# Attention and token/channel mixer: transposing u of batches 1 to 3 by DMA instead of on TensorE

## The chip, the cores and the metric

The kernel runs on one core of one Trainium2 chip. The metric is the device time of one execution in microseconds (us). Times of before: 226.68, 228.03 and 229.67 us in three runs, median 228.03. The profiled execution took 226.8 us.

Engines are named as in the profile: PE (TensorE), PEld (its weight loads), DVE (VectorE), ACT (ScalarE), POOL (GpSimd), SP (SyncE, which here only issues DMAs).

## The reference, cut

```python
# q, k, v: (4, 8, 768, 64); attention with 4 sink tokens and a window of 128
scores = scale * np.matmul(q, k.transpose(0, 1, 3, 2))
...
keep = is_sink | in_window
...
x = softmax(scores) @ v                 # then (4, 768, 512): batch, token, channel
xt = x.transpose(0, 2, 1)
h = np.maximum(xt @ w_tok1, 0.0) @ w_tok2
u = x + h.transpose(0, 2, 1)            # token mixing, residual
h2 = np.maximum(u @ w_ch1, 0.0) @ w_ch2
out = u + h2                            # channel mixing, residual; float32
```

## The kernel before, in words

There are 4 batches, and 16 pairs of heads, four pairs to a batch. Tokens are in 6 tiles of 128, channels in 4 tiles of 128. Each pair is loaded (load_qk, L75, from SP; load_v, L101, from POOL), cast to bf16 on POOL, transposed on PE, scored against its band and its sinks, put through exp on ACT, masked on DVE and multiplied with v (pv, L415). The result is x_sb, with tokens on the partitions.

Token mixing (mix_h, L474, and mix_u, L500) is done in two groups of channels: group 0 is the first 384 channels (three pairs of heads), group 1 the last 128 (the last pair). mix_u makes, for a token tile, two matmuls of 384 or 128 columns in PSUM (tag "mx", three banks), and DVE adds x (L513) and writes u_sb in bf16, with tokens on the partitions.

Channel mixing needs u with channels on the partitions: uT, a tile of 128 x 4 x 768. transpose_u (L522) makes it: PE transposes blocks of 128x128 of u_sb into PSUM (L114), and ACT or DVE copies them to uT (L118, L120). In a batch this is 24 blocks and 8 copies. Then mix_channels (L569) forms v1T = relu(w_ch1^T uT) in 12 tiles of channels and two halves of tokens of 384 each (a "half" is token tiles 0 to 2 or 3 to 5), four matmuls of 384 columns for each, one for each tile of channels; and then, per token tile, 12 matmuls of 512 columns with w_ch2 (out_part, L591), an addition of u on DVE (L603), and a store from SP (L606). u_sb, uT and h1T lie in two buffers, o_sb in three.

The order of the work is planned when the program is built. Plan (L223) keeps a clock for PE, ACT and DVE from written costs, and lets two streams of PE units run against each other: main is the channel mixing of batch b, side the attention and token mixing of batch b + 1. At each step it takes from the side stream if that is behind target(m) (L684), which says how much of the side should be done when main has come to m: before, all of it at 0.95 of main's stage. Every instruction is then kept in the planned order on its engine. Dependencies across engines, and for DMAs, are semaphores. A DMA has a lane of eight, and waits for the one that used that lane before it.

SP's queue is thus in planned order too: q and k loads, output stores, each behind the one before it. A store waits on SP for its addition on DVE. The loads of a pair are issued when the pair four earlier is through (load_next, L632).

The batch boundary is where main goes from batch b to b + 1: the 12 matmuls of mix_u of group 1 for batch b + 1, what is left of out_part for batch b and of attention for batch b + 2, then the first v1 of batch b + 1, which reads uT.

Of the kernel before, what the change touches and what calls it, by code (L numbers as in the profile page):

```python
# [16 lines left out]
def kernel(  # L17
# [13 lines left out]
    nc = tc.nc  # L31
    B, H, S, D = q.shape
    P = 128
    NT = S // P
# [5 lines left out]
    NTOK = DTOK // P  # L40
# [20 lines left out]
    in_order = tc.keep_in_program_order  # L61
# [66 lines left out]
    def load_w(out, in_):  # L128
# [15 lines left out]
        out=ident, in_=ident, compare_op=ALU.not_equal, fill=1.0, base=0, pattern=[[-1, P]], channel_multiplier=1,  # L144
    ))
    for i in range(2):
        in_order(nc.gpsimd.affine_select(
            out=mask_main[:, i, 0], in_=mask_main[:, i, 0], compare_op=ALU.is_ge,
# [3 lines left out]
            out=mask_main[:, i, 1], in_=mask_main[:, i, 1], compare_op=ALU.is_ge,  # L152
# [13 lines left out]
    for n in range(NKB):  # L166
        e = (nc.vector, nc.gpsimd)[n]
# [7 lines left out]
        out=mask_add, in0=mask_main, scalar1=-1.0, scalar2=30000.0, op0=ALU.add, op1=ALU.mult,  # L175
# [26 lines left out]
    for n in range(NW):  # L202
        ch1_last = load_ch1(n)

    class Op:
        def __init__(self, cost, fn, deps=(), tag=None, then=(), size=0.0):  # L210
            self.cost, self.fn, self.deps, self.tag, self.then = cost, fn, list(deps), tag, list(then)
            self.done = None
            self.size = size

    def landed(at):
# [1 line left out]
        op.done = at  # L217
        return op

    SEM = 90.0  # L220
    PE_OUT = 190.0

    class Plan:  # L223
        def __init__(self):
            self.free = {"PE": 0.0, "ACT": 0.0, "DVE": 0.0}
            self.pending = []
            self.rings = {t: [None] * n for t, n in TAGS.items()}
            self.turn = {t: 0 for t in TAGS}
# [43 lines left out]
        def run(self, main, side, target):  # L272

            main, side = list(main), list(side)
            m = s = 0.0
            while main or side or self.pending:
                o = self.other()
                tm = self.start_pe(main[0]) if main else None
                ts = self.start_pe(side[0]) if side else None
                pick = None  # L280
                if tm is not None and ts is not None:
                    behind = s < target(m)
                    if behind:
                        pick = "side" if ts <= tm + 40.0 else "main"
                    else:
                        pick = "main" if tm <= ts + 40.0 else "side"
                elif tm is not None:
                    pick = "main"
                elif ts is not None:
                    pick = "side"  # L290
                t = {"main": tm, "side": ts, None: None}[pick]
                if o is not None and (t is None or o[0] <= t):
                    op = self.pending.pop(o[1])
                    op.fn(o[2])
                    self.free[o[2]] = o[0] + op.cost[o[2]]
                    op.done = self.free[o[2]] + SEM
                    continue
                assert pick, "no unit can begin"
                if pick == "main":
                    op = main.pop(0)  # L300
                    m += op.size
                else:
                    op = side.pop(0)
                    s += op.size
                self.commit_pe(op, t)
# [10 lines left out]
    done = {}  # L316
    tiles = {}
# [149 lines left out]
    GROUPS = ((0, DM - P), (DM - P, P))  # L467
# [6 lines left out]
    def mix_h(b, g, t0, n):  # L474
        c0, cn = GROUPS[g]

        def run():
            if ("mix", b) not in tiles:
                tiles["mix", b] = (
                    mix_pool.tile([P, NTOK, DM], BF16, name="h1T"),  # L480
                    mix_pool.tile([P, NT, DM], BF16, name="u_sb"),
                    mix_pool.tile([P, NC, S], BF16, name="uT"),
                )
            ps_h = tiles["ps_h", b, g, t0] = bank("mx", n, cn)
            for tt in range(n):
                for st in range(NT):
                    mm(
                        ps_h[:, tt], w_tok1[:, st, ts(t0 + tt, P)], x_sb[b][:, st, c0:c0 + cn],
                        start=(st == 0), stop=(st == NT - 1),
                    )  # L490

        w = n * cn
        op = Op(
            {"ACT": 190.0 + 0.78 * w, "DVE": 150.0 + 1.05 * w},
            lambda e: relu(e, tiles["mix", b][0][:, t0:t0 + n, c0:c0 + cn], tiles["ps_h", b, g, t0]),
        )
        done.setdefault(("h", b, g), []).append(op)
        return unit(n * NT * cn * 0.422, run, of_group(b, g) + [done["tok1"]], "mx", [op])

    def mix_u(b, g, s0, n):  # L500
        c0, cn = GROUPS[g]

        def run():
            ps_u = tiles["ps_u", b, g, s0] = bank("mx", n, cn)
            for st in range(n):
                for tt in range(NTOK):
                    mm(
                        ps_u[:, st], w_tok2[:, tt, ts(s0 + st, P)], tiles["mix", b][0][:, tt, c0:c0 + cn],
                        start=(tt == 0), stop=(tt == NTOK - 1),
                    )  # L510

        def add(e):
            in_order(nc.vector.tensor_tensor(  # L513
                out=tiles["mix", b][1][:, s0:s0 + n, c0:c0 + cn], in0=tiles["ps_u", b, g, s0],
                in1=x_sb[b][:, s0:s0 + n, c0:c0 + cn], op=ALU.add,
            ))

        op = Op({"DVE": 150.0 + 1.05 * n * cn}, add)
        done["u", b, g, s0] = op
        return unit(n * NTOK * cn * 0.422, run, done["h", b, g] + [done["tok2"]], "mx", [op])  # L520

    def transpose_u(b, g, s0, n):  # L522
        ct0, nct = GROUPS[g][0] // P, GROUPS[g][1] // P

        def run():
            ps_ut = tiles["ps_ut", b, g, s0] = bank("tr", nct, n * P, dtype=BF16)
            for ct in range(nct):
                for st in range(n):
                    transpose(ps_ut[:, ct, ts(st, P)], tiles["mix", b][1][:, s0 + st, ts(ct0 + ct, P)])

        w = nct * n * P
        op = Op(
            {"ACT": 190.0 + 0.78 * w, "DVE": 150.0 + 0.52 * w},
            lambda e: copy(e, tiles["mix", b][2][:, ct0:ct0 + nct, s0 * P:(s0 + n) * P], tiles["ps_ut", b, g, s0]),
        )
        done.setdefault(("uT", b), []).append(op)
        return unit(nct * n * 56, run, [done["u", b, g, s0]], "tr", [op])

    def attention_and_tokens(b):
        p0 = b * NHP  # L540
        units = [transpose_q(p0), transpose_k(p0)]
        for p in range(p0, p0 + NHP):
            last = p == p0 + NHP - 1
            units += [score(p, 0), score(p, 1)]
            if not last:
                units.append(transpose_q(p + 1))
            if p > p0:
                units.append(pv(p - 1, 0))
            units += [score(p, 2), score(p, 3)]
            if not last:  # L550
                units.append(transpose_k(p + 1))
            units.append(score(p, 4))
            if p > p0:
                units.append(pv(p - 1, 1))
            units += [score(p, 5), score_sinks(p)]

            units[-1].then.append(sink_rows(p))
        units += [mix_h(b, 0, 0, 1), pv(p, 0), mix_h(b, 0, 1, 1), pv(p, 1)]
        for st in range(NT):
            units.append(mix_u(b, 0, st, 1))  # L560
            if st >= 2:
                units.append(transpose_u(b, 0, st - 2, 1))
        units += [
            mix_h(b, 1, 0, NTOK), transpose_u(b, 0, NT - 2, 1), mix_u(b, 1, 0, 4), transpose_u(b, 0, NT - 1, 1),
            mix_u(b, 1, 4, 2), transpose_u(b, 1, 0, 4), transpose_u(b, 1, 4, 2),
        ]
        return units

    def mix_channels(b):  # L569
# [84 lines left out]
    plan = Plan()  # L654
    plan.free.update(PE=3000.0, ACT=2200.0, DVE=3900.0)
    raw0 = raws.pop(0)
    for n, (name, at) in enumerate((("q_bf", 3900.0), ("k_bf", 5100.0))):
        done[name, 0] = Op(
            {"DVE": 550.0, "ACT": 830.0},
            lambda e, n=n: copy(e, bfs[0][n].rearrange("p j h d -> p h j d"), raw0[n]), [landed(at)],  # L660
# [23 lines left out]
    def target(m):  # L684
        m -= first
        total = 0.0
        for n, (msize, ssize) in enumerate(sizes):
            begin = 0.2 if n == 0 else 0.0
            f = (m / msize - begin) / (0.95 - begin)
            if f < 1.0 or n == B - 1:  # L690
                return total + max(0.0, min(1.0, f)) * ssize if m < msize else total + ssize
            if m < msize:
                return total + ssize
            total += ssize
            m -= msize
        return total

    plan.run(main, side, target)


# [33 lines left out]
```

## Time and profile before

| | |
|---|---|
| median of three runs | 228.03 us |
| profiled execution, own time | 226.8 us |
| its span, first to last instruction | 225.1 us |
| PE busy | 206.8 us of the span, 92% |
| DVE, ACT busy | 134.0 us, 128.1 us |
| granted TensorE clock | 1.00 |
| chain that ended last | PE 79%, DMA 10%, DVE 5%, ACT 2% |
| boundaries: first v1 of batch 1, 2, 3 | about 90, 140 and 190 us |

A span of an execution is cut in views: busy time of each engine in a stretch; groups of instructions with count, busy time and the mean length of one; the chain, which follows the last instruction back through whatever released each step; waits; and DMA issues with the time to landing. Matmuls on PE are pipelined, so the length of one is more than the step from one to the next. Rows of the SP queue give the time for which an issue held the queue.

### The profile page before, as it was taken

How to read it: one execution, taken by the hardware profiler on the slowest of the kernel's cores; microseconds unless marked ns; L12 is line 12 of the kernel's file. 1: busy time of each engine (PE TensorE's matmuls, PEld its weight loads, DVE VectorE, ACT ScalarE, POOL GpSimd, SP SyncE). 2: the span in 40 equal slices, each digit the busy share in tenths (PEclk: the TensorE clock that was granted, in tenths of full speed). 3: DMA queues.
4: the chain of work that ended last, by engine and by line, in shares of the span. 5: the costliest groups of instructions: out<-in, count | busy, mean ns of one | idle time of the engine just before them, and what ended most of it. 6: DMA issues, size and time to landing. Idle time of an engine off the chain costs nothing.

```text
span 225.1 us, 4435 instructions
## 1 busy us (share of the span) xinstructions
PE 206.8 (92%) x1770; PEld 132.5 (59%) x1788; DVE 134.0 (60%) x308; ACT 128.1 (57%) x259; POOL 53.1 (24%) x70
## 2 busy tenths in 40 slices
PE   1687896999999999999999999999999999999993
PEld 0455654666766656667766566667765566565441
DVE  5378975029899684499995554599964645000231
ACT  2687944689777522888884023889975022775000
POOL 8798461423045151001341600000000000000000
PEclk9999999999999999999999999999999999999999
DMA  6999999998088792670558921100001211100222
GB/s 198 302 192 154 205 185 260 259 212 260 24 127 171 145 296 60 194 272 4 35 38 153 150 98 47 48 3 0 3 0 50 85 56 50 47 0 0 96 93 93
DMA packets 41781, 26.24 MB, mean 117 GB/s; under 512 B 25888, under 2 KB 38688, under 8 KB 41760
## 3 DMA queue, kind: packets, MB, share of 16 engines
q0 software_dynamic: 29600, 7.08, 33.1%
q1 hardware_dynamic: 12160, 18.88, 25.1%
q8 instruction: 14, 0.23, 0.4%
q14 instruction: 7, 0.06, 0.1%
HBM read 26.74 MB, written 6.29 MB: 147 GB/s over the span
## 4 chain that ended last, share of the span: by engine, by line
PE 79%; DMA 10%; DVE 5%; ACT 2%; issue 1%; POOL 1%; SPq 0%; POOLq 0%
PE ps_mx L111 61%; PE ps_sc L111 8%; PE ps_tr L114 6%; DMA w_ch<-in_moe_w_ch_dram 5%; PE ps_pv L111 4%; DMA q_f<-in_q_dram 3%; DMA k_f<-in_k_dram 2%; DVE o_sb L603 1%; ACT kTz L118 1%; DVE pT L390 1%; DVE kTz L120 1%; ACT pT L384 1%; DVE x_sb L442 0%; POOL q_bf L95 0%; POOL w_ch L129 0%
## 5 line engine op out<-in xcount | busy, mean ns | idle before, releaser
L111 PE MATMUL ps_mx<-w_ch,v1T 128*128 128x512 bf16 x272 | 69.3, 379 | 1.1
L111 PE MATMUL ps_mx<-uT,w_ch 128*128 128x384 bf16 x384 | 69.6, 326 | 0.1
L384 ACT ACTIVATE pT<-ps_sc 128x512 bf16<-128x512 f32 x84 | 46.6, 565 | 10.7 <-PE ps_sc L111 9.3
L111 PEld LDWEIGHTS <-w_ch 128*128 128x128 bf16 x384 | 36.9, 98 | 21.5
L124 ACT ACTIVATE v1T<-ps_mx 128x384 bf16<-128x384 f32 x69 | 33.8, 490 | 12.7 <-PE ps_mx L111 11.9
L111 PEld LDWEIGHTS <-v1T 128*128 128x128 bf16 x288 | 27.0, 98 | 23.6 <-issue 0.7
L603 DVE TENSOR_TENSOR o_sb<-ps_mx,u_sb 128x512 f32<-128x512 f32 x24 | 16.6, 691 | 36.1 <-PE ps_mx L111 34.3
L111 PE MATMUL ps_sc<-qT,kTz 128*128 128x256 bf16 x168 | 31.0, 270 | 4.0 <-DVE kTz L120 1.7
L104 POOL DMA_DIRECT2D v_aug<-in_v_dram x16 | 16.8, 1049 | 58.2 <-PE ps_sc L111 35.7
L390 DVE TENSOR_TENSOR pT<-pT,mask_main 128x512 bf16<-128x512 bf16 (+1 forms) x68 | 29.2, 438 | 0.9
L111 PEld LDWEIGHTS <-kTz 128*128 128x128 bf16 x192 | 17.6, 101 | 14.8 <-DVE kTz L120 3.9
L118 ACT ACTIVATE uT<-ps_tr 128x384 bf16<-128x384 bf16 (+2 forms) x18 | 9.0, 502 | 29.6 <-PE ps_tr L114 29.6
L126 DVE TENSOR_SCALAR v1T<-ps_mx 128x384 bf16<-128x384 f32 x27 | 14.9, 556 | 13.3 <-PE ps_mx L111 12.9
L513 DVE TENSOR_TENSOR u_sb<-ps_mx,x_sb 128x384 bf16<-128x384 f32 (+2 forms) x32 | 16.7, 552 | 6.7 <-PE ps_mx L111 6.5
L111 PEld LDWEIGHTS <-w_tok 128*128 128x128 bf16 x192 | 14.6, 98 | 7.3 <-issue 0.8
L111 PEld LDWEIGHTS <-pT 128*128 128x128 bf16 x352 | 16.9, 97 | 3.1 <-issue 0.9
L118 ACT ACTIVATE kTz<-ps_tr 64x768 bf16<-64x768 bf16 x22 | 17.6, 799 | 1.2 <-PE ps_tr L114 1.0
L111 PE MATMUL ps_pv<-v_aug,pT 128*128 128x65 bf16 x304 | 16.4, 194 | 0.0
L95 POOL CAST q_bf<-q_f 128x768 bf16<-128x768 f32 x15 | 12.9, 863 | 12.3 <-DMA q_f<-in_q_dram 12.3
L442 DVE TENSOR_TENSOR x_sb<-ps_pv,recip 128x384 bf16<-128x384 f32 x28 | 15.5, 552 | 0.3
L111 PE MATMUL ps_mx<-h1T,w_tok 128*128 128x384 bf16 (+1 forms) x96 | 14.9, 272 | 0.5 <-ACT h1T L124 0.3
L120 DVE COPY qT<-ps_tr 128x768 bf16<-128x768 bf16 x12 | 11.5, 956 | 5.8 <-PE ps_tr L114 5.7
(57 smaller groups left out, 197.5 us busy)
## 6 DMA issues: line engine op xcount, KB each, us to landing
q_f<-in_q_dram SPq DMA_DIRECT2D x16, 384.0 KB, 5.8
k_f<-in_k_dram SPq DMA_DIRECT2D x16, 384.0 KB, 6.4
out_dram<-o_sb SPq DMA_DIRECT2D x24, 256.0 KB, 2.0
v_aug<-in_v_dram POOLq DMA_DIRECT2D x16, 192.0 KB, 6.5
w_ch<-in_moe_w_ch_dram POOLq DMA_DIRECT2D x8, 384.0 KB, 11.7
w_tok<-in_moe_w_tok_dram POOLq DMA_DIRECT2D x2, 384.0 KB, 5.8
```

The costliest lines, as they stand in the source:

```text
L104: d = in_order(nc.gpsimd.dma_start(out=v_aug.rearrange("p i t d -> p (i t) d")[:, :, 0:D], in_=v[b].rearrange("h s d -> (h s) d")[2 * hp * ...
L111: in_order(nc.tensor.matmul(*args, skip_group_check=True, **kwargs))
L114: in_order(nc.tensor.transpose(out, in_, ident))
L118: in_order(nc.scalar.activation(out, in_, AF.Copy))
L120: in_order(nc.vector.tensor_copy(out=out, in_=in_))
L124: in_order(nc.scalar.activation(out, in_, AF.Relu))
L126: in_order(nc.vector.tensor_scalar_max(out=out, in0=in_, scalar1=0.0))
L384: in_order(nc.scalar.activation(tiles["pT", p][:, kt, :, 0:nq], tiles["ps_s", p, kt][:, :, 0:nq * P], AF.Exp, scale=scale,))
L390: in_order(nc.vector.tensor_tensor(out=pt, in0=pt, in1=msk[:, :, 0:nq], op=ALU.mult))
L442: in_order(nc.vector.tensor_tensor(out=x_sb[b][:, ts(half, QH), ts(hp, 2 * D)].rearrange("p t (i d) -> p t i d", i=2), in0=tiles["ps_o", p ...
L513: in_order(nc.vector.tensor_tensor(out=tiles["mix", b][1][:, s0:s0 + n, c0:c0 + cn], in0=tiles["ps_u", b, g, s0], in1=x_sb[b][:, s0:s0 + n ...
L603: in_order(nc.vector.tensor_tensor(out=o_sb, in0=tiles["ps_out", b, st], in1=tiles["mix", b][1][:, st], op=ALU.add,))
```

## The change

For batches 1 to 3 transpose_u is replaced by transfer_u: per group and token tile one transposing DMA from u_sb to uT, issued from SP. Its PE units and copies go. Batch 0 is as before. The plan gets a clock for SP, a written cost of 500 ns for an issue and a lag of 2500 ns until uT counts as there. The side stream's target is now 0.85 of main's stage in place of 0.95. The two orders on PE are the same up to the token mixing of batch 1.

```diff
+    DMA_LAG = 2500.0
...
-            self.free = {"PE": 0.0, "ACT": 0.0, "DVE": 0.0}
+            self.free = {"PE": 0.0, "ACT": 0.0, "DVE": 0.0, "SP": 0.0}
...
-                    op.done = self.free[o[2]] + SEM
+                    op.done = self.free[o[2]] + op.lag
...
+    def transfer_u(b, g, s0, n):
+        ct0, nct = GROUPS[g][0] // P, GROUPS[g][1] // P
+        for st in range(s0, s0 + n):
+            def run(e, st=st):
+                _, u_sb, uT = tiles["mix", b]
+                in_order(nc.sync.dma_start(
+                    out=uT[:, ct0:ct0 + nct, ts(st, P)], in_=u_sb[:, st, ts(ct0, P)] if nct == 1 else
+                    u_sb[:, st, ct0 * P:(ct0 + nct) * P], transpose=True,
+                ))
+
+            op = Op({"SP": 500.0}, run, [done["u", b, g, s0]], lag=DMA_LAG)
+            done.setdefault(("uT", b), []).append(op)
+            plan.pending.append(op)
...
-        for st in range(NT):
-            units.append(mix_u(b, 0, st, 1))
-            if st >= 2:
-                units.append(transpose_u(b, 0, st - 2, 1))
-        units += [
-            mix_h(b, 1, 0, NTOK), transpose_u(b, 0, NT - 2, 1), mix_u(b, 1, 0, 4), transpose_u(b, 0, NT - 1, 1),
-            mix_u(b, 1, 4, 2), transpose_u(b, 1, 0, 4), transpose_u(b, 1, 4, 2),
-        ]
+        if b == 0:
...
+        else:
+            for st in range(NT):
+                units.append(mix_u(b, 0, st, 1))
+                transfer_u(b, 0, st, 1)
+            units.append(mix_h(b, 1, 0, NTOK))
+            for s0, n in ((0, 4), (4, 2)):
+                units.append(mix_u(b, 1, s0, n))
+                transfer_u(b, 1, s0, n)
...
-            f = (m / msize - begin) / (0.95 - begin)
+            f = (m / msize - begin) / (0.85 - begin)
```

In the changed program's order, SP has for each of the batches 1 to 3 six transposing DMAs of 128x384 (group 0) and six of 128x128 (group 1). For batch 1: six of group 0, three of group 1, the store of output tile 5 of batch 0, three of group 1, the store of tile 6, then loads. For batches 2 and 3: two of group 0, the store of tile 3 of the batch before, four of group 0, the store of tile 4, two of group 1, the store of tile 5, four of group 1, the store of tile 6. Between the last mix_u and the first matmul that reads uT, PE has 18 w_ch matmuls before each batch, and before batches 1 and 2 also transposes and scores of the next batch's attention.

More of the change, by code (lines that the diff above doesn't have):

```diff
@@ L203, with __init__ @@
         ch1_last = load_ch1(n)
+    SEM = 90.0
+    PE_OUT = 190.0
+    DMA_LAG = 2500.0
     class Op:
-        def __init__(self, cost, fn, deps=(), tag=None, then=(), size=0.0):
+        def __init__(self, cost, fn, deps=(), tag=None, then=(), size=0.0, lag=None):
             self.cost, self.fn, self.deps, self.tag, self.then = cost, fn, list(deps), tag, list(then)
             self.done = None
+            self.lag = SEM if lag is None else lag
             self.size = size
@@ L218, in landed @@
         return op
-    SEM = 90.0
-    PE_OUT = 190.0
     class Plan:
         def __init__(self):
-            self.free = {"PE": 0.0, "ACT": 0.0, "DVE": 0.0}
+            self.free = {"PE": 0.0, "ACT": 0.0, "DVE": 0.0, "SP": 0.0}
             self.pending = []
@@ L558, in attention_and_tokens @@
         units += [mix_h(b, 0, 0, 1), pv(p, 0), mix_h(b, 0, 1, 1), pv(p, 1)]
-        for st in range(NT):
-            units.append(mix_u(b, 0, st, 1))
-            if st >= 2:
-                units.append(transpose_u(b, 0, st - 2, 1))
-        units += [
-            mix_h(b, 1, 0, NTOK), transpose_u(b, 0, NT - 2, 1), mix_u(b, 1, 0, 4), transpose_u(b, 0, NT - 1, 1),
-            mix_u(b, 1, 4, 2), transpose_u(b, 1, 0, 4), transpose_u(b, 1, 4, 2),
-        ]
+        if b == 0:
+            for st in range(NT):
+                units.append(mix_u(b, 0, st, 1))
+                if st >= 2:
+                    units.append(transpose_u(b, 0, st - 2, 1))
+            units += [
+                mix_h(b, 1, 0, NTOK), transpose_u(b, 0, NT - 2, 1), mix_u(b, 1, 0, 4), transpose_u(b, 0, NT - 1, 1),
+                mix_u(b, 1, 4, 2), transpose_u(b, 1, 0, 4), transpose_u(b, 1, 4, 2),
+            ]
+        else:
+            for st in range(NT):
+                units.append(mix_u(b, 0, st, 1))
+                transfer_u(b, 0, st, 1)
[3 more added lines that the diff above has]
+                transfer_u(b, 1, s0, n)
         return units
```

## The prediction

> **What bounds the kernel now.** I read the busy shares first, then the busy times of three stretches, one per batch boundary to the next, then the chain around two boundaries, then the rows for DMA issues. The first view says which engine is full over the whole span, the second whether it is full where the change acts.
>
> ```profile
> PE 206.8 (92%) x1770; PEld 132.5 (59%) x1788; DVE 134.0 (60%) x308; ACT 128.1 (57%) x259; POOL 53.1 (24%) x70
> ```
>
> ```profile
> 40.15:91.43 51.28, 50.59 (x452) 33.10 (x455) 33.81 (x74) 33.01 (x69) 16.82 (x19) 1.00 0.82 166
> 91.43:141.63 50.20, 49.74 (x441) 32.56 (x445) 35.83 (x81) 29.82 (x61) 10.45 (x12) 1.00 0.53 111
> 141.63:189.00 47.37, 47.02 (x419) 30.86 (x422) 32.62 (x79) 28.80 (x59) 0.00 (x0) 1.00 0.09 33
> ```
>
> Each row is a stretch, its length, then busy us of PE, its weight loads, DVE, ACT, POOL, then the granted clock (1.00 all through), DMA share and GB/s. Of 148.85 us PE is idle for 0.69 + 0.46 + 0.35 = 1.5 us. So PE bounds all three, and whatever leaves PE's stream there shortens the span, as long as no new wait comes in. The removed transposes lie there:
>
> ```profile
> L114 PE MATMUL ps_tr<-ident,u_sb 128*128 128x128 bf16 x72 | 7.9, 219 | 0.4 <-DVE u_sb L513 0.4
> ```
>
> A mean of 219 ns is the length of one, but they are pipelined; what one costs is its step in the chain. This is the chain before the last boundary (start, length, what):
>
> ```profile
> 184.47 1.24 PE ps_mx L111 x5
> 185.71 0.17 PE ps_tr L114 x3
> 185.87 1.09 PE ps_mx L111 x11
> 186.97 0.17 PE ps_tr L114 x3
> 187.14 0.87 PE ps_mx L111 x7
> 188.01 0.22 PE ps_tr L114 x4
> 188.23 0.65 PE ps_mx L111 x3
> 188.88 0.11 PE ps_tr L114 x2
> 188.99 17.11 PE ps_mx L111 x103
> ```
>
> Three transposes take 0.17, four 0.22, two 0.11 us: 56.5 ns each. The same view prices the matmuls: 0.216 us for one of 512 columns (three: 0.65), 0.163 for 384, 56.5 ns for 128. All copies of uT are over before the 103 matmuls begin, and PE waits for none. The DMA rows I use (shortest/median/longest ns on the SP queue, then us to landing), first the output stores, then the loads of q and k:
>
> ```profile
> L606 SPq DMA_DIRECT2D out_dram<-o_sb x24: 332/333/360, 64.7 to 222.2; - x24
> DMA to landing us min/median/max: 2.0/2.0/5.3
> ```
>
> ```profile
> L81 SPq DMA_DIRECT2D q_f<-in_q_dram x16: 367/420/1068, 0.8 to 119.7; - x16
> L81 SPq DMA_DIRECT2D k_f<-in_k_dram x16: 397/455/997, 1.3 to 120.2; - x16
> DMA to landing us min/median/max: 3.0/6.3/9.4
> ```
>
> **The change, part by part.** *Removed.* Batches 1 to 3 lose 4 x 6 transposes each, 72 in all, with weight loads that run beside PE: 72 x 56.5 ns = 4.07 us off PE's chain. Their 24 copies (uT rows of 0.29 to 0.60 us) leave ACT and DVE; since PE was idle for only 1.5 us in the three stretches, their absence can give 1.5 us at the very most, and I count nothing.
>
> *Added.* 36 transposing DMAs on SP: per batch six of 128x384 (group 0) and six of 128x128 (group 1). None is in the trace, so two numbers are unknown: I, the time that one holds the SP queue, and L, from issue to landing. Bounds: I from 0.33 (store) to 1.07 us (longest load); L from 2.0 (stores, which also read SBUF) up to 5.3 (longest store), and below 2.0 is possible, since nothing here is written to HBM. I take I = 0.46 (loads) and L = 2.0, the row nearest in source and size: DMA is light around the two later boundaries (0.19 in that column from 129 to 140.5 us and from 178.7 to 190), and 0.78 around the first, where the loads of 74.7 to 77 us are landing. Small packets speak for a longer L: in the software queue 29600 packets took 33.1% of 16 engines, 40 ns each. If a transpose moves rows of 256 bytes one by one, 128x128 makes 8 per engine (0.3 us) and 128x384 makes 24 (1.0 us): small beside 2.0.
>
> *What waits.* PE is in order. In the changed order the first matmuls of a batch wait for uT: half 0 for the token tiles 0 to 2, half 1 for tiles 3 to 5, the fourth matmul of each for group 1. Group 1's DMAs are the last, and SP is in order too: the store of output tile 5 stands among them, and waits for its addition on DVE. Set t = 0 at the start of the first eight group-1 matmuls of mix_u. Before, at the last boundary, the addition behind eight of them starts 0.65 us after they start and takes 0.69: 1.34. The second addition (0.42) ends at 1.76. The twelve matmuls end at 0.68.
>
> - Boundary before batch 3: 18 matmuls of w_ch follow (3.89), nothing else, as no attention is left. Needed: half 0 at 0.68 + 3.89 + 0.49 = 5.06, half 1 at 5.71. Tile 5 is summed after six of the 18, at 1.98; addition 0.2 later, to 2.87; store issued 2.92 to 3.25; then four transposes (tiles 2 to 5). Tile 2 lands at 3.25 + L = 5.25, tile 5 at 3.25 + 3I + L = 6.63. PE waits 0.2, and then 6.63 - 5.9 = 0.7: **0.9 us**.
> - Before batch 2: the same store, but PE has 6 w_ch, 12 transposes of q and k, 12 w_ch, 4 scores, 6 transposes, 2 scores = 5.57 us. Needed 6.74 and 7.39; landing 5.25 and 6.63. Covered, by 0.8 us.
> - Before batch 1: 5.37 us of such work, needed 6.54 and 7.19. Six transposes of q go ahead of tile 5's last matmuls, so its store ends at 3.6 and three transposes follow: 3.6 + 2I + L = 6.5. Covered, by 0.7 us.
>
> So only the last boundary pays, and the other two start to pay at about 0.8 us more.
>
> *Moved: the second edge at boundary 1.* Before, transposes filled PE while DVE added u:
>
> ```profile
> 80.49 2.41 DVE L513 TENSOR_TENSOR u_sb<-ps_mx,x_sb 128x384 bf16<-128x384 f32 x5
> 81.10 0.34 PE L114 MATMUL ps_tr<-ident,u_sb 128*128 128x128 bf16 x3 [0.43 <-DVE u_sb L513]
> ```
>
> Now twelve matmuls of mix_u stand in one row there. They have three banks, and a bank is freed at DVE's pace, 2.41 / 5 = 0.48 us, while two matmuls take 0.33. Pairs 4 to 6 and the mix_h behind them start at 81.10, 81.58, 82.07 and 82.54: 1.44 us for 0.98 us of work. I charge 0.5 us. At the other boundaries w_ch matmuls stand between, and I charge nothing.
>
> *Moved: SP and side stream.* On SP, loads of q and k for batch 3 stand behind batch 1's transposes, but behind the store of tile 6 in both orders, so they leave at about the same time. Group 0's DMAs come one per 0.48 us, from t = -3.5 at boundary 1 (where the chain has the first addition end at 81.05), and need 0.46: no backlog. The target 0.85 packs the attention of batches 2 and 3 tighter (that of batch 1 keeps its order). PE was idle there for 0.6 us outside the boundaries; doubling half of that I charge as 0.3 us; the ends are 0 and 3.
>
> **Sum:** 226.8 - 4.07 + 0.9 + 0.5 + 0.3 = 224.4 us against the profiled execution's own time of 226.8 (span 225.1 and 1.7 around it). The runs of before were 226.68, 228.03 and 229.67, so this execution was near the fastest, 1.2 under the median. I add half of that: 225.0.
>
> **The rivals.**
> *Landing or issue is longer (the other side).* Place: the DMAs behind the store of tile 5 and the first group of v1T. With I kept at 0.46, the three waits are 3.25 + 3I + L - 5.71, the same - 7.39, and 3.6 + 2I + L - 7.19, in sum 3L - 6.5. Without them the change is worth 4.07 - 0.5 - 0.3 = 3.3 us, so it is level at L = 3.3 and slower by 2% (4.5 us) at L = 4.8. A longer I weighs more: at I = 1.0, group 0 of boundary 1 ends at -3.5 + 6 = 2.5, three of group 1 at 5.5, the store at 5.8 and the last lands at 7.8 + L; at the other two the store goes at 3.37 and the last lands at 6.7 + L. With L = 2.0 the waits are 2.6 + 1.3 + 3.0 = 6.9, the time 226.8 - 3.3 + 6.9 = 230.4; with L = 3.0 (shortest load) 233.4; with L = 5.3, 240. For it: loads took up to 1.07 us on SP and never landed under 3.0. Against: those came from HBM in bursts, at a DMA share of 0.82 in the first of the three stretches.
> *Transposes run one at a time.* If each must land before the next, at 2.0 us, group 0 alone takes 12 us. At boundary 1 (start t = -3.5) the twelfth ends at 20.5 and PE waits 13.3 us; at the other two four of group 0 begin at t = -5.3 and end at 2.7, and six more end at 14.7: waits of 7.3 and 9.0. Time: 226.8 - 3.3 + 29.6 = 253. For it: nothing in this trace. Against: ordinary DMAs on SP overlap, loads leave every 0.5 us and land after 6. The Trainium skill, "VectorE: DVE Perf Modes", section "The three transpose paths", gives 390 ns for a 128x128 on TensorE and 1309 ns by DMA, and its rules for authors choose TensorE where PSUM will do as the target. TensorE's is 219 ns in this trace; the DMA's is shown by no run yet. By that page 24 blocks one after another would be 31 us a batch, the waits of this rival 44 us and its time 268 (an estimate from the page).
> *Everything is hidden and the freed DVE and ACT help too.* No wait at the boundaries, and the 1.5 us of idle PE gone: 226.8 - 4.07 - 1.5 = 221.2. Against: the store of tile 5 holds the last four back by its own addition even if L is short.
>
> That the change does not do what it says can be left out: PE has 72 transposes less in the changed order.
>
> **How the numbers follow.** Forecast 0.55 (222.7 to 227), longer landing or issue 0.27 (226.8 to 240, two thirds of it over 2%), one at a time 0.08, all hidden 0.10 (six of ten over 2%). About 2% is what a measurement of this kernel can tell from no change. Faster by over 2%: 0.06. Slower: 0.18 + 0.08 = 0.26. Within: 0.68. The range 222 to 238 leaves out "one at a time", the longest landings and the best of the hidden case, under 2 in 10.
>
> **What would show it.** The transposes' rows on SP give I and L at once. PE's group for u_sb should have 24 transposes left. PE's idle time before its uT matmuls, put down to the transposing DMA, should be near 1 us, nearly all of it before batch 3; 0.5 us should be put down to DVE's u_sb before batch 1. I am wrong if a wait for uT shows before each batch, if I is above 1 us, or if SP's stores keep DVE's additions waiting.

## The result, and the profile after

The changed kernel took 249.02 us (median of 4 runs, 248.03 to 250.33) against 228.85 for the kernel before in the same job (4 runs, 226.68 to 230.96): a ratio of 1.092, interval 1.080 to 1.104. It is slower, and far above the forecast of 225.0. The profiled execution after took 249.82 us, its span 248.1.

From part 1 and part 2 of the page of after, PE's busy time and the granted clock over the span:

```profile
PE 212.6 (86%) x1699; PEld 131.2 (53%) x1716; DVE 130.9 (53%) x292; ACT 121.9 (49%) x251; POOL 53.2 (21%) x70
...
PEclk9999997999999998599999999799999996599999
```

PE has 72 transposes less to do (71 fewer matmul records) and is busy for 5.8 us *more* (206.8 before). The second line says why. In before all forty digits are 9:

```profile
PEclk9999999999999999999999999999999999999999
```

In after there are lower ones: the 7 at about 40 us lies in the start (on which below), but 85, 7 and 65 lie where the batches change. Some of PE's work ran at a lower clock.

The wait that the prediction priced at 0.9 us, from the waits of after (who, for what: sum us, times, longest):

```profile
PE ps_mx L111 <- DMA uT<-u_sb: 16.3, 6, 3.4
```

The rows of the new DMAs, from the view of their source line (hold of the SP queue in ns: shortest, median, longest; then us from issue to landing):

```profile
L530 SPq DMA_TRANSPOSE uT<-u_sb x36: 1099/1213/2387, 82.5 to 208.5; - x36
...
DMA to landing us min/median/max: 2.2/2.4/6.0
```

So I, the hold, is 1.21 us, where the prediction took 0.46 and an upper bound of 1.07; L, the landing, is 2.4 us, where it took 2.0. The chain of after at the boundary before batch 1 (start, length, what) shows what that does:

```profile
94.26 0.52 SPq L632
94.79 0.04 issue
94.83 1.11 SPq L530
95.94 0.04 issue
95.98 1.23 SPq L530
97.22 0.04 issue
97.26 2.33 DMA uT<-u_sb
99.59 0.04 issue
99.63 3.04 PE ps_mx L111 x9
```

SP works without a pause: the store (L632), then transposes 1.2 us apart, and PE starts 0.04 us behind the landing of the last one. A landing of 2.33 us is longer than the hold, so the next transpose leaves before the last one has landed; what PE waits for is the sum of the holds and one landing. The same place on PE (start, length, instructions, idle time before them and its releaser):

```profile
95.47 0.81 PE L111 MATMUL ps_mx<-uT,w_ch 128*128 128x384 bf16 x4 [2.93 <-DMA uT<-u_sb]
99.63 3.04 PE L111 MATMUL ps_mx<-uT,w_ch 128*128 128x384 bf16 x9 [3.35 <-DMA uT<-u_sb]
```

The other four waits are 1.10 and 3.04 us before batch 2, 3.40 and 2.49 before batch 3: per boundary 6.3, 4.1 and 5.9. Nine matmuls of 384 columns took 3.04 us, 0.34 each, where the trace of before had 0.163. The next view, busy time in stretches of after, shows it (stretch, length, busy us of PE, PEld, DVE, ACT, POOL, granted clock, DMA share, GB/s):

```profile
97.60:104.40 6.80, 4.77 (x17) 2.54 (x18) 0.00 (x0) 2.49 (x5) 0.00 (x0) 0.50 0.68 220
155.60:159.00 3.40, 3.40 (x12) 1.72 (x13) 0.00 (x0) 1.36 (x3) 0.00 (x0) 0.50 0.15 55
206.80:217.00 10.20, 7.39 (x23) 3.27 (x23) 0.00 (x0) 2.76 (x6) 0.00 (x0) 0.50 0.12 35
```

Right at or behind each wait the clock is 0.50, for 6.8, 3.4 and 10.2 us. PE was busy for 4.77 + 3.40 + 7.39 = 15.6 us in them; at full clock half of that would do, so 7.8 us are lost. Of these, 0.7 cost nothing. Before batch 3 four of the slow matmuls run ahead of the last wait, and at full clock PE would only have waited that much longer for the last landing:

```profile
207.12 1.44 PE L111 MATMUL ps_mx<-uT,w_ch 128*128 128x384 bf16 x4 [3.40 <-DMA uT<-u_sb]
```

So the half clock adds 7.8 - 0.7 = 7.1 us to waits that would be 16.3 + 0.7 = 17.0 at full clock.

**The account.** The first 80 us differ between executions whose PE order is the same up to there (the fourth output store was issued at 79.9 us before and 81.4 after), so I compare the *rest*: from that issue to the end of the span. Before it is 145.2 us, after 166.7, in the traces 21.5 more. Of that: -4.07 for the 72 transposes, +16.3 waits for uT, +7.8 half clock, +0.4 for DVE's pace at boundary 1: 20.4. About 1 us stays unassigned. The 0.4 is read here:

```profile
82.53 1.41 PE L111 MATMUL ps_mx<-h1T,w_tok 128*128 128x384 bf16 x6 [0.43 <-DVE u_sb L515]
83.92 0.83 PE L111 MATMUL ps_mx<-x_sb,w_tok 128*128 128x128 bf16 x12
```

From 82.53 to 83.92 are 1.39 us for six matmuls that are 0.98 us of work. The idle 0.43 ahead of them is no part of it: it stands in before as well.

Medians below are of all executions and ratios of undisturbed ones alone; the profiled execution of store_on_act was a disturbed one, so of it only waits and issue times are read.

### The profile page after: what moved, and what is told of

Read it like the earlier page. It is cut to its first block, busy times and chain, and to the rows that moved or that the text cites. A ratio compares the mean times of both kernels' runs of the same rounds, so it can differ in the third digit from the quotient of the medians.

```text
span 248.1 us, 4335 instructions
## 1 busy us (share of the span) xinstructions
PE 212.6 (86%) x1699; PEld 131.2 (53%) x1716; DVE 130.9 (53%) x292; ACT 121.9 (49%) x251; POOL 53.2 (21%) x70
## 4 chain that ended last, share of the span: by engine, by line
PE 71%; DMA 12%; SPq 8%; DVE 3%; ACT 2%; issue 2%; POOL 1%; POOLq 0%
PE ps_mx L111 56%; PE ps_sc L111 7%; SPq L530 7%; DMA w_ch<-in_moe_w_ch_dram 5%; PE ps_pv L111 4%; PE ps_tr L114 4%; DMA q_f<-in_q_dram 3%; DMA uT<-u_sb 3%; DVE o_sb L629 2%; DMA k_f<-in_k_dram 2%; ACT kTz L118 1%; SPq L632 1%; DVE kTz L120 1%; ACT pT L386 1%; DVE k_bf L120 0%
## 5 line engine op out<-in xcount | busy, mean ns | idle before, releaser
L111 PE MATMUL ps_mx<-uT,w_ch 128*128 128x384 bf16 x384 | 78.7, 353 | 16.3 <-DMA uT<-u_sb 16.3
L111 PE MATMUL ps_mx<-w_ch,v1T 128*128 128x512 bf16 x273 | 67.2, 379 | 1.0
L111 PEld LDWEIGHTS <-w_ch 128*128 128x128 bf16 x384 | 39.1, 105 | 43.5 <-issue 26.1
L629 DVE TENSOR_TENSOR o_sb<-ps_mx,u_sb 128x512 f32<-128x512 f32 x24 | 16.6, 691 | 49.7 <-PE ps_mx L111 49.6
L111 PEld LDWEIGHTS <-kTz 128*128 128x128 bf16 x192 | 18.1, 101 | 17.0 <-DVE kTz L120 4.0
L124 ACT ACTIVATE h1T<-ps_mx 128x384 bf16<-128x384 f32 (+1 forms) x12 | 5.5, 455 | 32.3 <-PE ps_mx L111 32.3
L515 DVE TENSOR_TENSOR u_sb<-ps_mx,x_sb 128x384 bf16<-128x384 f32 (+2 forms) x32 | 16.1, 550 | 8.7 <-PE ps_mx L111 8.7
L118 ACT ACTIVATE kTz<-ps_tr 64x768 bf16<-64x768 bf16 x19 | 15.2, 800 | 3.8 <-PE ps_tr L114 3.2
L111 PE MATMUL ps_pv<-v_aug,pT 128*128 128x65 bf16 x304 | 16.3, 194 | 0.0
L111 PE MATMUL ps_mx<-h1T,w_tok 128*128 128x384 bf16 (+1 forms) x96 | 14.1, 272 | 0.9 <-DVE u_sb L515 0.4
L95 POOL CAST k_bf<-k_f 128x768 bf16<-128x768 f32 x15 | 13.3, 886 | 4.4 <-DMA k_f<-in_k_dram 4.4
```

The costliest lines, as they stand in the source:

```text
L95: in_order(nc.gpsimd.tensor_copy(out=t.rearrange("p j h d -> p h j d"), in_=f))
L111: in_order(nc.tensor.matmul(*args, skip_group_check=True, **kwargs))
L118: in_order(nc.scalar.activation(out, in_, AF.Copy))
L124: in_order(nc.scalar.activation(out, in_, AF.Relu))
L515: in_order(nc.vector.tensor_tensor(out=tiles["mix", b][1][:, s0:s0 + n, c0:c0 + cn], in0=tiles["ps_u", b, g, s0], in1=x_sb[b][:, s0:s0 + n ...
L629: in_order(nc.vector.tensor_tensor(out=o_sb, in0=tiles["ps_out", b, st], in1=tiles["mix", b][1][:, st], op=ALU.add,))
```

## The experiments

My theory (A): a transposing DMA holds SP for about 1.2 us whatever its size, up to some size; a batch has twelve, with stores among them, and PE waits for the end of that queue; waits of about 3 us then bring the half clock. Rivals: (B) the hold goes by blocks moved, so that fewer and larger DMAs gain nothing; (C) the stores, which wait for DVE in SP's queue, make the delay; (D) the target 0.85 does. "Before" is run beside each, with a median between 229.2 and 229.7 us. The table has the numbers of all runs; ratios are against before, and "rest" is the stretch defined above. Six medians lie outside the range that was expected, by 0.7 to 3.2 us: pe_85, merged_g1, hybrid_85, fill_waits and merged_all_95 above it, store_on_act below it (dma_70, further off, is taken up in its place). Where a gain or a loss is under 2%, the argument goes by waits, holds and rests.

| kernel | median us | ratio, interval | waits for uT, us | rest, us |
|---|---|---|---|---|
| before | | 1 | none | 145.2 |
| after | 249.02 | 1.092 (1.080 to 1.104) | 16.3 | 166.7 |
| pe_85 | 229.81 | 1.004 (0.999 to 1.009) | none | 145.2 |
| dma_95 | 256.15 | 1.122 (1.112 to 1.133) | 17.1 | 171.1 |
| dma_70 | 244.05 | 1.063 (1.056 to 1.070) | 11.2 | 160.6 |
| fill_waits | 244.25 | 1.066 (1.060 to 1.072) | 2.0 | 159.6 |
| store_on_act | 242.32 | 1.046 (1.036 to 1.056) | 7.8 | |
| split_24 | 297.27 | 1.296 (1.285 to 1.306) | 57.4 | 212.4 |
| hybrid_85 | 229.22 | 0.997 (0.990 to 1.005) | none | 143.8 |
| merged_g1 | 228.25 | 0.999 (0.994 to 1.004) | 1.8 | 143.7 |
| merged_all | 226.00 | 0.985 (0.977 to 0.992) | none | 141.6 |
| merged_all_again | 224.37 | 0.978 (0.972 to 0.985) | none | 141.6 |
| one_per_group | 226.01 | 0.981 (0.974 to 0.989) | none | 141.7 |
| merged_all_95 | 230.88 | 1.008 (1.001 to 1.015) | 1.6 | 146.8 |

**pe_85, dma_95, dma_70: the target alone.** The kernel before with 0.85 (pe_85), and the changed one with 0.95 and 0.70 in the same line. The edit of pe_85:

```diff
-            f = (m / msize - begin) / (0.95 - begin)
+            f = (m / msize - begin) / (0.85 - begin)
```

> The kernel before with the target at 0.85, all transposes on PE. Theory A: the target costs nothing by itself, 225 to 229, PE idle between 40 and 189 us no more than 2 us. Rival D (the tighter side stream is part of the loss): PE idle in the batches grows, 232 or more.

> The changed kernel with the target back at 0.95. Theory A: less work of main is left behind the last mix_u, about 3 us less per boundary, so the waits grow from 16.3 to some 24 us, and the time to 255 to 260. Rival D (the target is part of the loss): 240 to 247.

> The changed kernel with the target at 0.70. Its order leaves 42 matmuls of w_ch behind the last mix_u before batches 2 and 3 (24 more, 5.2 us), and keeps the boundary before batch 1. Theory A: the wait before batch 1 stays at 6.3 us, the others fall from 4.1 and 5.9 to 0 and about 0.7, with their half clock: 233 to 238. Rival D (a tighter side stream costs PE by itself): the same waits, but idle time of PE within the batches grows by some us: 239 or more.

With PE's transposes the target costs nothing: the same rest to 0.1 us, so D falls. With the DMAs 0.95 costs 4.4 us more of the rest and 0.70 gives 6.1 back. Neither is as I expected in its waits. At 0.95 they are 17.1 and not some 24, and 3.0 us of waits for copies of k come beside them. At 0.70 waits of 11.2 us stay. An earlier side stream also puts the additions of u closer together: before batches 2 and 3 they span 7.2 and 5.6 us in place of 9.2. The queue counts from the first of them and hardly shrinks: from its first transpose to its twelfth it takes 15.9 and 15.3 us, against 16.6 and 17.0 in after.

**merged_g1: group 1 in two DMAs in place of six.** Four and two token tiles each; DVE writes group 1 to a tile of its own, contiguous along tokens, and POOL copies it to u_sb for the output addition.

```diff
-                transfer_u(b, 1, s0, n)
+                transfer_many(b, 1, s0, n)
...
+            in_order(nc.sync.dma_start(
+                out=uT[:, ct0, s0 * P:(s0 + n) * P].rearrange("p (s q) -> p s q", q=P),
+                in_=tiles["u1", b][:, s0:s0 + n].rearrange("p s q -> p (s q)"), transpose=True,
+            ))
```

> The changed kernel with group 1's six transposing DMAs of a batch made two (four token tiles, then two). For that, DVE writes group 1 of u into a tile of its own, and POOL copies it into u_sb; nothing is left out. Theory A (each transposing DMA holds the SP queue 1.2 us whatever its size, and the sum of these holds is what PE waits for): the two DMAs hold SP about 1.2 us each, the waits before batches 1 to 3 fall from 16.3 us to under 2, the clock stays at 1.0, time 223 to 227. Rival B (the hold goes with the blocks moved): the DMA of four tiles holds SP near 4.8 us, waits and time stay, 246 to 250.

The holds, from the views of the two lines of merged_g1 (group 1: two and four tiles of 128x128; group 0: one of 128x384), and its wait:

```profile
L548 SPq DMA_TRANSPOSE uT<-u x6: 1195/1206/1229, 92.4 to 190.8; - x6
```

```profile
L534 SPq DMA_TRANSPOSE uT<-u_sb x18: 1187/1207/1862, 84.5 to 187.6; - x18
```

```profile
PE ps_mx L111 <- DMA uT<-u: 1.8, 3, 1.1
```

Four tiles hold the queue as long as one did. B falls for these sizes. Four holds less before each boundary take the waits from 16.3 to 1.8 us, and with the longest at 1.14 us the granted clock is 1.00 in the stretches around all three boundaries.

**split_24: the same bytes in twice as many DMAs,** 24 of 128x128 in a batch.

```diff
         for st in range(s0, s0 + n):
+            for ct in range(ct0, ct0 + nct):
...
+                        out=uT[:, ct:ct + 1, ts(st, P)], in_=u_sb[:, st, ts(ct, P)], transpose=True,
```

> The changed kernel with group 0's DMAs of 128x384 split by tile of channels: 24 transposing DMAs of 128x128 per batch in place of 12, the same bytes. Theory A: twelve more holds of 1.2 us, some 14.5 us more of queue at each of three boundaries: the waits grow by about 44 us, 290 to 300 with the clock. Rival B (blocks count, not DMAs): 246 to 252.

From the view of its line and its waits:

```profile
L531 SPq DMA_TRANSPOSE uT<-u_sb x72: 1093/1230/2647, 85.4 to 257.9; - x72
```

```profile
PE ps_mx L111 <- DMA uT<-u_sb: 57.4, 8, 16.3
```

For group 0 a third of the size, and the same hold. Twelve more DMAs a batch cost 297.3 - 249.0 = 48 us, 1.34 us for each of the 36 more, which is a hold and a little; 57.4 - 16.3 = 41.1 us of it are waits for uT.

**hybrid_85: group 0 by DMA, group 1 on PE as before.** This leaves six DMAs a batch, all with attention still to cover them.

```diff
-                transfer_u(b, 1, s0, n)
+            units += [transpose_u(b, 1, 0, 4), transpose_u(b, 1, 4, 2)]
```

> The changed kernel with group 1 of batches 1 to 3 transposed on PE again (after mix_u, as before), group 0 by DMA. Theory A: only six DMAs of 1.2 us per batch, all issued before group 1 is summed, so no wait for uT; 54 x 56.5 ns = 3.05 us less on PE than before: 223 to 226. Rival C (any transposing DMA next to the stores and loads is slow to land, or the target 0.85 is what costs): waits of several us stay before each batch, 235 or more.

No wait for uT, and the rest is 1.4 us shorter. 54 transposes fewer should be worth 54 x 56.5 ns = 3.05 us; where the other 1.7 go I did not trace, beyond the 0.4 of DVE's pace. In the runs the gain can't be told from nothing.

**fill_waits: the half clock alone.** 27, 18 and 26 extra matmuls with the identity, whose result nobody reads, before the first v1 of batches 1 to 3: PE is busy while it waits.

```diff
+                if b and ft == 0 and half == 0:
+                    ps_fill = bank("tr", DM)
+                    for _ in range((0, 27, 18, 26)[b]):
+                        mm(ps_fill, ident, w_ch2[:, 0], start=True, stop=True)
```

> The changed kernel with idle-time matmuls on PE (27, 18 and 26 of 512 columns, on data that is read by nobody) between the last work ahead of each batch boundary and the first matmul that reads uT: 5.8, 3.9 and 5.6 us of work, a little less than the waits of 6.3, 4.1 and 5.9. They add work and change no result. Theory E (the rows after each wait run at half the clock because PE had stood idle): the clock stays at 1.0 past the boundaries and some 7.5 us go, time 240 to 243. Rival F (the clock falls there whatever PE does, or the filling only delays): 248 or more.

The clock and the wait of fill_waits:

```profile
PEclk9999998899999999999999999999999999999999
```

```profile
PE ps_mx L111 <- DMA uT<-u_sb: 2.0, 2, 1.0
```

With PE kept busy, the clock stays up past all three boundaries (the 88 lies in the start), and the rest falls by 7.1 us, though the filler does nothing to bring a transfer sooner. That is the net cost of the half clock worked out above: it is caused by the idle time and is paid on top of it.

**store_on_act: the stores leave SP's queue.**

```diff
-                in_order(nc.sync.dma_start(out=out[b, ds(st * P, P)], in_=o_sb))
+                in_order(nc.scalar.dma_start(out=out[b, ds(st * P, P)], in_=o_sb))
```

> The changed kernel with the output stores issued from ACT's queue in place of SP's. Rival G (what the prediction put first: the store of tile 5, which waits for DVE, holds the last transposes back): the waits fall by 3 us and more at each boundary, time 238 or less. Theory A (the twelve holds of 1.2 us are the length of the queue; a store among them adds only its 0.5 us): the last transpose of a batch leaves 1 to 1.5 us earlier, the waits fall by 3 to 5 us in all, 243 to 247.

Its waits from 85 us on:

```profile
PE ps_mx L111 <- DMA uT<-u_sb: 7.8, 4, 3.1
...
PE ps_sc L111 <- ACT kTz L118: 3.8, 3, 2.7
```

The waits for uT halve, but ACT's queue now holds the stores that wait for DVE, and PE waits for ACT's copies of k, 3.8 us that after does not have there and that put off the need for uT. The queue on SP shows what the stores themselves cost: from the first transpose of a batch to its twelfth it took 14.75, 14.5 and 15.1 us, in after 14.75, 16.6 and 17.0. So it became shorter by 0, 2.0 and 1.9 us, within the 3 to 5 in all that theory A expected. The stores (C) are a part of the delay, not its body: twelve transposes without stores still end too late.

**merged_all and merged_all_again: five DMAs a batch.** Group 0 by pairs of token tiles (three DMAs), group 1 by four and two; u and uT of batches 1 to 3 in a tile for each group, without POOL's copy; the output addition in two DVE instructions, one a group. The second run is the same kernel in another job.

```diff
-                transfer_u(b, 0, st, 1)
+                if st % 2:
+                    transfer_many(b, 0, st - 1, 2, (st - 1, st))
...
-                transfer_u(b, 1, s0, n)
+                transfer_many(b, 1, s0, n, (s0,))
```

> The changed kernel with five transposing DMAs per batch in place of twelve: group 0 by pairs of token tiles (48 blocks of 16 x 128 each), group 1 as four and two tiles. For that u and uT of batches 1 to 3 lie in a tile per group, and the output addition is two DVE instructions. Nothing is left out. Theory A (1.2 us a hold whatever the size): no wait for uT at any boundary, 4.07 us less on PE less 0.5 at the first boundary, 224 to 226, or 143 us or less behind the fourth output store. Rival B2 (a hold stays at 1.2 us only up to some size): the DMAs of 48 blocks hold SP longer, 2.4 us.

> The kernel of merged_all once more, with more rounds: faster than before by 1 to 2%, the interval clear of 1.

From the view of its line in merged_all, two, four or six blocks of 128x128 in a DMA (the expectations count in blocks of 16x128, eight to one of 128x128), and PE's waits from 79 us on:

```profile
L548 SPq DMA_TRANSPOSE uT<-u x15: 1195/1218/1792, 82.0 to 185.1; - x15
```

```profile
PE ps_mx L111 <- DVE u L517: 0.4, 1, 0.4
PE ps_mx L111 <- DVE o_sb L651: 0.4, 2, 0.2
```

No wait for uT is left, and the rest is 3.6 us shorter than before. That agrees with the prediction's gain without waits, 4.07 - 0.5. Both runs are faster than before, by 1.5 and 2.2%, with intervals clear of 1 but not of 2%. The new layout of u and the split output addition were not run without the merging, so what they do by themselves is not shown.

**one_per_group: two DMAs a batch,** six token tiles each, 18 and six blocks of 128x128.

```diff
+                if st == NT - 1:
+                    transfer_many(b, 0, 0, NT, range(NT))
...
+            transfer_many(b, 1, 0, NT, (0, 4))
```

> The kernel of merged_all with one transposing DMA per group and batch: 144 blocks for group 0, 48 for group 1, issued when the last addition is done. Theory A: two holds of about 1.2 us, no wait for uT except perhaps under 1 us before batch 3; 223 to 227. Rival B2 (a hold grows beyond some size): group 0's DMA holds SP for several us (144 blocks at the 0.05 us that 1.2 / 24 gives: 7 us), and before batch 3 PE waits for 1 to 4 us: 227 to 232.

```profile
L548 SPq DMA_TRANSPOSE uT<-u x6: 1228/2072/3782, 83.7 to 183.9; - x6
...
DMA to landing us min/median/max: 2.8/3.9/6.3
```

The three of six blocks hold SP for 1.23 to 1.47 us, the three of 18 for 2.68, 2.70 and 3.78. So B has something in it between six and 18 blocks, but PE waits for none of them here.

**merged_all_95: the best version with the old target.**

```diff
-            f = (m / msize - begin) / (0.85 - begin)
+            f = (m / msize - begin) / (0.95 - begin)
```

> The kernel of merged_all with the target at 0.95 as before. Its last DMA of a batch leaves about 3 us after the addition and lands 2.4 later; at 0.95 some 3 us less of main is left to cover it: a wait of 0 to 2 us per boundary, 225 to 230. If theory A is wrong on the landing, no change: 226.

Its rest is 5.1 us longer than with 0.85: waits of 1.6 us for uT come back, and 3.0 us of scores waiting for copies of k. So the target of 0.85, which cost nothing in pe_85, is a help to the DMAs.

## Why the prediction was wrong, step by step

- **The 4.07 us for 72 transposes**: borne out. merged_all, which leaves them out and does not wait for uT, has 3.6 us less rest, close to 4.07 less the 0.5 charged for DVE's pace.
- **The 0.5 us for DVE's pace**: right in place and size, 0.4 in after. The sign named for it was not: 0.43 us put down to DVE's u_sb stand in before as well, and the loss lies within PE's busy time.
- **I = 0.46 us, bounds 0.33 to 1.07**: this is the step that failed. It was taken from ordinary loads because nearest in source and size; a transpose is another kind of instruction (DMA_TRANSPOSE in the rows, loads are DMA_DIRECT2D), and its hold was 1.21, above even the upper bound. The row of loads bounds only loads. With "need 0.46: no backlog" fell the rest: at 1.26 us from one to the next, group 0 of batch 1 ends at -3.5 + 6 x 1.26 = 4.06, three of group 1 at 7.84, the store at 8.4, and the last transpose starts at 10.92 and lands at 13.3, where it is needed at 7.19: a wait of 6.1 us. The same sum gives 10.6 against 7.39 and 5.71 for batches 2 and 3: 3.2 and 4.9. Together 14.2 us. Measured, per boundary, 6.3, 4.1 and 5.9, together 16.3. The sum over the queue was sound, this input was not. The prediction named I above 1 us, and a wait before each batch, as signs of being wrong; both came.
- **L = 2.0 us**: 2.4 measured. Small: 0.4 us a boundary.
- **"The store of tile 5 holds the last four back"**: it was put first among the causes, and comes behind the holds. It is true that a store stands among them (0.52 us in the chain), and taking the stores off SP takes 8.5 us off the waits for uT. But the queue became shorter by only 3.9 us in all, PE waited 3.8 us for copies of k instead, and 7.8 are left; with fewer transposes and all stores in place, none.
- **"Covered, by 0.8 us", "by 0.7 us"**: these margins held only for I = 0.46, and the prediction said that the other two boundaries would pay from about 0.8 us more. They did.
- **The clock was not in the sum at all.** This is the second step that failed, a cost put at nothing. The trace of before, with forty nines, gave no warning; the page of the Trainium skill on the clock gate, cited in the last section, does. The rival "longer landing or issue" lacked it too: with 1.26 us from one transpose to the next its sum gives 226.8 - 3.3 + 14.2 = 237.7; adding the net 7.1 gives 244.8, against 249.8 for the profiled execution. Of the 5.0 left, 1.4 lie before the fourth store and 2.8 in waits that were longer than in this sum (17.0 at full clock against 14.2).
- **"One at a time", 253 us**, was close in number and wrong in its mechanism: it had 29.6 us of waits from landings of 2.0 us in a row. Transposes left 1.2 us apart and landed 2.4 us after their issue, and the time is made of 16.3 us of waits and 7.8 of clock.
- **The target, 0.3 us**: 0 in pe_85.

The Trainium skill, "VectorE: DVE Perf Modes", section "The three transpose paths", has 1309 ns for a 128x128 by DMA and its rules choose TensorE where PSUM will do. The measured hold for one of 128x128 is 1.2 us, close to it (to its landing it took 2.2 to 2.4). But up to four blocks of 128x128 in one DMA cost the same hold and six cost 1.33 us, so here the price went by the instruction and not by the block. With twelve small DMAs a batch TensorE was the faster, as the rule has it; with five larger ones it was the slower, by about 2%.

What stays open: what takes the 1.2 us within SP's issue, and about 1 us of the 21.5. Transposes from a second queue were not tried.

## What to carry to other kernels

Price a DMA on its queue by its kind and its count, not by its bytes (that held here up to six blocks of 128x128 in one), and if no row of the trace has that kind, let the upper end be far above the nearest row. When work leaves an engine that is always busy for one that answers later, add up the queue from the first producer to the last consumer, and then add the clock: 16.3 us of idle gaps cost another 7.1 us of half clock here. Merge such DMAs until the queue fits under the work that covers it; here that was done by laying out u contiguously for each group.

## What the hardware showed that I had not expected

- A transposing DMA from SBUF to SBUF held SP for 1.20 to 1.23 us at the median with one to four blocks of 128x128 in it (after, split_24, merged_g1), for 1.33 us with six (1.21 to 1.79, merged_all), and for 2.7 to 3.8 us with 18 (one_per_group). Stores took up to 0.53 us in after, 0.33 to 0.36 before.
- The clock. PE's matmuls that read uT took, in two stretches of after, right behind the wait and later (groups by form: count, then busy us, mean ns of one):

```profile
L111 PE MATMUL ps_mx<-uT,w_ch 128*128 128x384 bf16 x13 | 4.4, 510 | 3.4 <-DMA uT<-u_sb 3.4
```

```profile
L111 PE MATMUL ps_mx<-uT,w_ch 128*128 128x384 bf16 x77 | 14.7, 327 | 0.0
```

  The slow stretches of 3.4, 6.8 and 10.2 us are one, two and three times 3.4. Waits of 3.04 and 3.40 us brought the last two, and the first began within a wait of 3.35 us that followed one of 2.93. A wait of 1.14 us (merged_g1) and one of 2.25 (dma_70, before batch 2) brought none, but in dma_70 the clock also fell 2.1 us into a wait of 2.92: the length of a wait alone does not decide it. Nor need PE be idle altogether: it had run for 0.81 us of the 3.4 before the clock fell at 97.6 us, and in dma_70 for 1.27 before the fall at 95.3. The Trainium skill, "TensorE: Matmul & The Clock Gate", section "What's actually happening", has a free-running window of 3.4 us whose idleness halves the clock, and its table under "Why this matters for your kernels" warns of gaps over some 3 us; the trace agrees, with a window partly busy as an addition.
